# Eight of the down projection's 28 block products done by seven smaller products each: a second Strassen-Winograd level, in part

## The chip, the cores and the metric

One core of one Trainium2 chip. The metric is the device time of one execution in microseconds (us), lower is better.

## The reference

A linear attention block (A) and a gated block (B) run twice on 2048 tokens of width 1024. Only B's last matrix product, the down projection, changes:

```
x = x + A(layernorm(x));  x = x + B(layernorm(x));  x = x + A(layernorm(x));  x = x + B(layernorm(x))

def B(x, w_gate, w_up, w_down):          # D = 1024, F = 3584
    h = (x @ w_gate) * (x @ w_up)
    return h @ w_down                    # [2048, 3584] @ [3584, 1024]
```

Inputs and output are bfloat16.

## The kernel before

The kernel already uses one level of Strassen's scheme in Winograd's form: a product of 2x2 blocks is done with seven block products instead of eight, at the price of sums of blocks. Tokens are taken in two halves, so with two layers there are four **passes** of the down projection (I number them 1 to 4; each follows a gate/up stage), each with seven **products**, named in the order in which they run: 1, 2, 6, 7, 4, 5, 3. One product is [512 tokens x 1792] times [1792 x 512], 56 matmuls of 128x128 stationary (h) by 128x512 moving (weights). In code and traces PE is TensorE with its matmuls, PEld its weight loads, DVE VectorE, ACT ScalarE, POOL GpSimd; L1609 is line 1609 of the kernel; a bank is the part of PSUM into which the code sums a group of matmuls (`psb(bank)`); with a semaphore the program makes one engine wait for another. `...` marks cuts:

```python
DPROD = ["1", "2", "6", "7", "4", "5", "3"]
...
for qi, q in enumerate(DPROD):
    ...
    def grp(t, hf, ...):                    # t: 128 tokens, hf: half of the 14 slices of K
        bank = (B_DX if q in "1674" else B_DV)[t]
        P.add("pe", lambda e: [e.matmul(psb(bank), hv[:, 7 * hf + k, t * 128:(t + 1) * 128], w[:, k, :],
                                        start=(q in "15" and hf == 0 and k == 0), stop=(hf == 1 and k == 6), ...)
                               for k in range(7)], ...)
        if t == 3:
            ring_issue()                    # refill this weight slot
    for t in range(4):
        ...
        grp(t, 0); grp(t, 1)
        if q == "1":   ...  ACT copies the bank; DVE: hd += hc, ha = hd - ha
        elif q in "24": ... DVE: x = bank * CD + x
        elif q in "67": ... DVE: rtmp = bank * CD + x;  for 6 also hb -= ha, ha = hc - ha
        else:           ... DVE: x = bank * CD + rtmp
        ticks(q, t)                         # layernorm of the next stage, sums for the next pass
```

The program gives every engine its instructions in one fixed order; a helper works out which semaphores each must wait for. And `ha`, `hb`, `hd` are changed in place by VectorE in products 1 and 6, so in the program product 7 starts on a tile of tokens only when VectorE has got through its queue up to that tile.

## Time and profile before

| | before |
|---|---|
| time, median of 3 runs | 1462.43 us (1460.23 to 1463.21) |
| span of the profiled run | 1456.9 us |
| four passes, first to last start of their matmuls | 87.84, 88.51, 88.10, 88.10 us |
| spacing of starts, 128x512 (1553 pairs) / 128x256 (1884 pairs) | 0.2158 / 0.1092 us |

The engines' busy time from the page (busy us, share of the span, number of instructions):

```profile
PE 1437.1 (99%) x7850; PEld 755.1 (52%) x7850; DVE 1133.2 (78%) x2248; ACT 657.6 (45%) x1354; POOL 144.7 (10%) x176
```

Groups of the same trace: the down projection's matmuls, and below them, kept apart by shape, VectorE's sums of 1792 columns and the gate/up stage's half-width matmuls. The columns are busy us in all and mean ns of one, then the idle time of the engine just before them:

```profile
L1609 PE MATMUL ps<-arena 128*128 128x512 f16 (+1 forms) x1568 | 340.9, 379 | 0.0
...
L757 DVE TENSOR_TENSOR arena<-arena 128x1792 f16<-128x1792 f16 x64 | 69.0, 1084 | 1.2
...
L1392 PE MATMUL ps<-arena 128*128 128x256 f16 x2184 | 287.5, 273 | 1.9 <-DVE ps L1405 1.0 <-DMA arena<-sp_scratch 0.9
```

A matmul's 379 or 273 ns is its modelled length in the pipeline, not what it costs; what it costs in a stream is the spacing of the starts, 215.8 or 109.2 ns. The down projection's matmuls never wait: 0.0 us. In the chain of work that ended last each pass is a single piece (start us, length us, what), here the first and the last:

```profile
416.04 81.58 PE ps L1609 x378
...
1373.92 80.09 PE ps L1609 x371
```

So any matmul column taken out of a pass shortens the kernel by its own time, as long as nothing else becomes late. How busy the others are in the four passes shows in the windows (window, then its length and the busy us of each engine, with the number of instructions):

```profile
core 0: us, PE busy (x) PEld busy (x) DVE busy (x) ACT busy (x) POOL busy (x), PEclk, DMA share, GB/s
412.00:498.00 86.00, 86.00 (x400) 39.02 (x399) 45.47 (x59) 2.88 (x5) 4.67 (x4) 1.00 0.65 202
661.00:744.00 83.00, 83.00 (x388) 37.71 (x386) 57.09 (x92) 2.28 (x4) 11.11 (x21) 1.00 0.89 282
1121.00:1209.00 88.00, 88.00 (x415) 40.26 (x413) 47.52 (x64) 3.23 (x6) 4.67 (x4) 1.00 0.71 231
1367.00:1454.00 87.00, 86.99 (x408) 39.64 (x406) 37.96 (x49) 3.23 (x6) 0.00 (x0) 1.00 0.47 163
```

VectorE (DVE) is free for 26 to 49 us of each pass.

### The profile page before, as it was taken

How to read it: one execution, taken by the hardware profiler on the slowest of the kernel's cores; microseconds unless marked ns; L12 is line 12 of the kernel's file. 1: busy time of each engine (PE TensorE's matmuls, PEld its weight loads, DVE VectorE, ACT ScalarE, POOL GpSimd, SP SyncE). 2: the span in 40 equal slices, each digit the busy share in tenths (PEclk: the TensorE clock that was granted, in tenths of full speed). 3: DMA queues.
4: the chain of work that ended last, by engine and by line, in shares of the span. 5: the costliest groups of instructions: out<-in, count | busy, mean ns of one | idle time of the engine just before them, and what ended most of it. 6: DMA issues, size and time to landing. Idle time of an engine off the chain costs nothing.

```text
span 1456.9 us, 21047 instructions
## 1 busy us (share of the span) xinstructions
PE 1437.1 (99%) x7850; PEld 755.1 (52%) x7850; DVE 1133.2 (78%) x2248; ACT 657.6 (45%) x1354; POOL 144.7 (10%) x176
## 2 busy tenths in 40 slices
PE   8999998999999999999999999999999999999999
PEld 3444443455544466664444444446666445666544
DVE  6987977999964599987579878778888736888842
ACT  5673355444410166660047723567765004777400
POOL 2212521000010000001010045210000100000000
PEclk9999999999999999999999999999999999999999
DMA  8578977997785777768885166667776956777652
GB/s 260 88 202 224 214 177 153 301 302 269 258 269 187 244 255 247 258 238 266 257 267 137 58 169 163 173 177 258 259 243 202 328 190 225 260 257 252 224 185 94
DMA packets 270455, 320.17 MB, mean 220 GB/s; under 512 B 161936, under 2 KB 212880, under 8 KB 270352
## 3 DMA queue, kind: packets, MB, share of 16 engines
q1 hardware_dynamic: 270352, 318.82, 71.6%
q8 instruction: 62, 1.02, 0.3%
q14 instruction: 41, 0.34, 0.1%
HBM read 236.45 MB, written 73.40 MB: 213 GB/s over the span
## 4 chain that ended last, share of the span: by engine, by line
PE 86%; DVE 7%; DMA 3%; ACT 2%; issue 1%; POOL 1%; SPq 0%; ACTq 0%; DVEq 0%
PE ps L1311 27%; PE ps L1609 23%; PE ps L1392 16%; PE ps L1130 8%; PE ps L911 6%; PE ps L882 3%; PE ps L1232 2%; DMA arena<-arena 2%; DVE arena L443 2%; DVE arena L757 1%; DVE arena L604 1%; DMA arena<-in_A_wqkv_dram 1%; POOL arena L1013 1%; DMA arena<-sp_scratch 1%; PE ps L1156 0%
## 5 line engine op out<-in xcount | busy, mean ns | idle before, releaser
L757 DVE TENSOR_TENSOR arena<-arena 128x512 f16<-128x512 f16 (+10 forms) x951 | 430.2, 480 | 61.6 <-ACT arena L1396 34.1
L760 DVE SCALAR_TENSOR_TENSOR arena<-ps,arena 128x512 f16<-128x512 f32 (+2 forms) x497 | 336.3, 688 | 172.4 <-PE ps L1609 136.9
L1311 PE MATMUL ps<-arena 128*128 128x512 f16 x1888 | 457.3, 379 | 2.7 <-ACT ps L1340 2.0
L1609 PE MATMUL ps<-arena 128*128 128x512 f16 (+1 forms) x1568 | 340.9, 379 | 0.0
L1392 PE MATMUL ps<-arena 128*128 128x256 f16 x2184 | 287.5, 273 | 1.9 <-DVE ps L1405 1.0
L1311 PEld LDWEIGHTS ps<-arena 128*128 128x128 f16 (+1 forms) x1888 | 182.8, 98 | 165.6 <-ACT ps L1340 6.3
L1392 PEld LDWEIGHTS ps<-arena 128*128 128x128 f16 (+1 forms) x2184 | 212.1, 98 | 92.8 <-ACT arena L1396 6.9
L1609 PEld LDWEIGHTS ps<-arena 128*128 128x128 f16 x1568 | 153.4, 98 | 183.7
L1316 ACT ACTIVATE arena<-ps 128x512 f32<-128x512 f32 x224 | 133.7, 597 | 81.4 <-PE ps L1311 64.4
L1340 ACT COPY ps<-ps 128x512 f32<-128x512 f32 x112 | 65.4, 584 | 178.5 <-PE ps L1311 167.0
L1396 ACT ACTIVATE arena<-ps 128x256 f32<-128x256 f32 x351 | 125.1, 385 | 26.9 <-PE ps L1392 22.0
L911 PE MATMUL ps<-arena 128*128 128x512 f16 (+1 forms) x560 | 123.2, 379 | 2.7 <-ACT arena L918 0.9
L1130 PE MATMUL ps<-arena 128*128 128x512 bf16 x512 | 116.1, 379 | 0.0
L1232 PE MATMUL ps<-arena 128*128 128x512 bf16 x512 | 111.4, 379 | 3.6 <-ACT ps L1226 3.0
L446 POOL TENSOR_SCALAR arena<-arena 128x1 f32<-128x1 f32 x64 | 23.1, 360 | 810.3 <-DVE arena L445 810.3
L1402 ACT COPY ps<-ps 128x256 f32<-128x256 f32 x182 | 66.4, 365 | 75.0 <-DVE arena L760 28.3
L443 DVE BATCH_NORM_STATS2 arena<-arena 128x6 f32<-128x512 bf16 x128 | 88.2, 689 | 13.8 <-DMA arena<-in_A_x_dram 7.0
L1013 POOL TENSOR_TENSOR arena<-arena 128x1024 f16<-128x1024 f32 x32 | 75.3, 2354 | 183.4 <-DVE arena L1011 166.3
L911 PEld LDWEIGHTS ps<-arena 128*128 128x128 f16 x560 | 54.0, 98 | 70.9 <-ACT arena L918 5.1
L882 PE MATMUL ps<-arena 128*128 128x512 bf16 x384 | 85.5, 379 | 3.7 <-ACT arena L547 1.6
L1405 DVE TENSOR_TENSOR ps<-ps,arena 128x256 f32<-128x256 f32 x182 | 76.7, 428 | 10.5 <-PE ps L1392 9.6
L1232 PEld LDWEIGHTS ps<-arena 128*128 128x128 f16 x512 | 49.8, 98 | 64.8 <-ACT ps L1226 4.3
(56 smaller groups left out, 755.3 us busy)
## 6 DMA issues: line engine op xcount, KB each, us to landing
arena<-w_scratch SPq DMA_DIRECT2D x84, 896.0 KB, 4.6
arena<-t_scratch SPq DMA_DIRECT2D x32, 896.0 KB, 6.1
arena<-in_B_w_down_dram SPq DMA_DIRECT2D x24, 896.0 KB, 5.0
arena<-sp_scratch SPq DMA_DIRECT2D x26, 768.0 KB, 4.2
w_scratch<-arena SPq DMA_DIRECT2D x28, 512.0 KB, 6.2
arena<-w_scratch SPq DMA_DIRECT2D x28, 384.0 KB, 5.2
x_scratch<-arena SPq DMA_DIRECT2D x40, 256.0 KB, 7.6
arena<-x_scratch SPq DMA_DIRECT2D x40, 256.0 KB, 5.6
```

Source lines behind the costliest of these rows:

```text
L443: P.add("dve", (lambda h: lambda e: e.bn_stats(st[j][:, 6 * h:6 * h + 6], x_res[:, i, (D // 2) * h:(D // 2) * (h + 1)]))(h), rd=r_x(i, (D ...
L757: P.add("dve", lambda e: e.tensor_tensor(out=out, in0=a, in1=b, op=op), rd=rd, wr=wr, prd=prd)
L760: P.add("dve", lambda e: e.scalar_tensor_tensor(out=out, in0=a, scalar=sc, in1=b, op0=ALU.mult, op1=op1), rd=rd, wr=wr, prd=prd)
L882: return [e.matmul(psb(bank), xnT[:, k, i * 128:(i + 1) * 128], t[:, k, h * 512:(h + 1) * 512], start=(k == 0), stop=(k == KT - 1)) for k ...
L911: P.add("pe", lambda e: [e.matmul(psb(bank), a[0][:, k, :], b[0][:, k, :], start=(q in (1, 5) and k == 0), stop=(k == 3), skip_group_check ...
L1130: return [e.matmul(psb(bank), xrt[t][:, jj * 128:(jj + 1) * 128], pk[:, h, t, :], start=(t == tok[0]), stop=(t == tok[NST - 1])) for t in ts]
L1232: return [e.matmul(psb(bank), xnT[:, g, i * 128:(i + 1) * 128], wp[:, g, dh * 512:(dh + 1) * 512], start=(dh == 0 and g == 0), stop=(g == ...
L1311: P.add("pe", lambda e: [e.matmul(psb(bank), w[:, k, :], x[:, k, :], start=(start and k == 0), stop=(k == 3), skip_group_check=True) for k ...
L1316: P.add("act", lambda e: e.activation(t, psb(bank), AF.Copy, scale=SG), prd=[bank], wr=r)
L1392: P.add("pe", lambda e: [e.matmul(psb(bank)[:, 256 * half:256 * half + 256], w[:, k, :], xx[:, k, :], start=(start and k == 0), stop=(k == ...
L1396: P.add("act", lambda e: e.activation(d, src, AF.Copy, scale=sc), prd=[xk], wr=rd_)
L1609: P.add("pe", lambda e: [e.matmul(psb(bank), hv[:, 7 * hf + k, t * 128:(t + 1) * 128], w[:, k, :], start=(q in "15" and hf == 0 and k == 0 ...
```

## The change

Products 4 and 5 (passes 1 and 3), 5 (pass 2), and 4, 5 and 3 (pass 4), eight of the 28, are each done by seven sub-products again: 98 matmuls of 128x256 in place of 56 of 128x512, an eighth fewer columns. VectorE makes four sums of h (S1 to S4) and four of the weights (T1 to T4) ahead of time, each 128x1792, at points named in a schedule: "20" is after tile 0 of product 2, "4d" after step d of product 4, the steps being the twelve entries of `order`. The sub-results are put together in PSUM and SBUF by VectorE and ScalarE. The four sums of h's input for the next pass (`tq`) move from product 5 to product 3, because their buffers now hold S sums.

The diff, cut to its core (`...` marks cuts; buffers and the re-ordering of the plain branch into `evac` are left out):

```diff
+    L2DOWN = {(False, 0): "45", (False, 1): "5", (True, 0): "45", (True, 1): "453"}
+    DSCHED = {
+        "45": {"20": "S1:5 S1:4", "21": "S2:5 S2:4", "22": "S3:5 S4:4", "23": "S4:5", "70": "S3:4 T1:4", "72": "T2:4 T3:4", "73": "T1:5",
+               "4d": "T4:4", "4j": "T2:5", "4m": "T3:5", "5d": "T4:5"},
+        "5": {"20": "S1:5", "21": "S2:5", "22": "S3:5", "23": "S4:5", "41": "T1:5", "42": "T2:5", "43": "T3:5", "5d": "T4:5"},
+        "453": {"20": "S1:5 S1:4", ..., "23": "S4:5", "70": "S3:4 T1:4", "71": "S1:3", "72": "T2:4 T3:4", "73": "T1:5",
+                "4d": "T4:4", "4f": "S2:3", "4j": "T2:5", "4m": "T3:5", "5d": "T4:5 S4:3", "5h": "T1:3", "5k": "S3:3", "5m": "T2:3", "3d": "T3:3", "3f": "T4:3"},
+    }
...
+                    l2w[q] = dict(ops={"S1": (s1, a21, a22, ALU.add), "S2": (s2, s1, a11, ALU.subtract), "S3": (s3, a11, a21, ALU.subtract),
+                                       "S4": (s4, a12, s2, ALU.subtract), "T1": (t1, b12, b11, ALU.subtract), "T2": (t2, b22, t1, ALU.subtract),
+                                       "T3": (t3, b22, b12, ALU.subtract), "T4": (t4, b21, t2, ALU.subtract)},
+                                  mm={1: (a11, b11), 2: (a12, b21), 3: (s4, b22), 4: (a22, t4), 5: (s1, t1), 6: (s2, t2), 7: (s3, t3)}, done=[])
+                def l2_ops(q, step):
+                    for tk in sched.get(q + str(step), "").split():
...
+                        tt(o[0], a[0], b[0], op, a[1] + b[1], o[1])
...
+                    def mm(i, r, bank, half, start=False):
+                        (a, ra), (b, rb) = W["mm"][i]
+                        P.add("pe", lambda e: [e.matmul(psb(bank)[:, 256 * half:256 * half + 256], a[:, k, 128 * r:128 * r + 128], b[:, k, :],
+                                                        start=(start and k == 0), stop=(k == 6), skip_group_check=True) for k in range(7)], ...)
...
+                    def first_(r):
+                        mm(5, r, UB[r], 0, True)
+                        mm(1, r, UB[r], 1)
+                        if q == "5":
+                            P.add("act", ... r4 = copy of half 0 ...)
+                            put(r, r)                 # ACT: half 1 into the result's bank
+                        else:
+                            acc(r, 1, r, 0, rin)      # DVE: three half-width accumulations
+                            acc(r + 2, 1, r, 0, rin)
+                            acc(r, 0, r, 1, rin)
+                    def m6(r):
+                        mm(6, r, UB[r], 1)
+                        put5(r, r)  or  acc(r, 1, r, 1, rout)
+                    def m7(r):
+                        mm(7, r, UB[r], 1)
+                        put5(r + 2, r); put(r + 2, r)  or  two acc
...
+                    order = ((f, 0), (f, 1), (m2, 0), (m6, 0), (m2, 1), (m6, 1), (m7, 0), (m3, 0), (m7, 1), (m3, 1), (m4, 0), (m4, 1))
+                    for st_, (fn, r) in enumerate(order):
+                        fn(r)
...
+                        l2_ops(q, "abcdefghijkm"[st_])
...
-                if q == "5":
+                if q == "3" and t < 2:
+                    tq.pop(0)()
                     tq.pop(0)()
```

## The prediction

> **What bounds the kernel now.** TensorE's stream of matmuls. The engine table gives PE 99% of 1456.9 us, DVE 78%, ACT 45%; the chain that ended last is 86% PE. PE is never late in the stage that changes: the groups table gives the down projection's matmuls (1568 of 128x512) 0.0 us of idle before them, and the chain runs through each of the four passes as one unbroken piece of 80 to 82 us (about 412-497, 661-745, 1125-1210, 1371-1455 us). Starts in the timeline are 0.2158 us apart for a 128x512 matmul and 0.1092 us apart for a 128x256 one (gate/up stage, 1884 pairs, although each loads its own 128x128 weights, 98 ns). So halving the width costs only about 1% of the rate. [...]
>
> **Removed and added, per changed product.** Before: 56 matmuls x 0.2158 = 12.09 us of PE. After: 7 x 2 x 7 = 98 matmuls x 0.1092 = 10.70 us. Saved 1.39 us; eight products: 11.1 us, 0.76% of the span. All of it lies on the chain.
>
> Added on DVE: eight sums of 128x1792 f16; the same shape takes 1.08 us in the groups table (1.065 back to back), 8.6 us. Products 4 and 3 also need 12 half-width accumulations (a 128x512 one takes 0.69 us, so I estimate 0.42 us for 128x256, 0.36 back to back): 4.5-5 us. Product 5 needs four PSUM additions (0.43 us) and six ACT copies (0.37 us). In all about 69 + 19 + 7 = 95 us of DVE, lifting it to some 85% of the span. DMA traffic is unchanged, ring refills move by about 1 us, and the four half-transformed sums of the next pass (1.22 us each) move from product 5 to product 3.
>
> **Does DVE fit?** By windows, DVE is busy in the four passes about 39-44, 58, 47 and 37 us of 84. Added: 22, 10, 22 and 35. So it fits on average. Locally: product 2 of pass one gets 7.5 us of sums behind a DVE backlog that already lasts until 431 us; I get about 2 us of lag, absorbed in product 7, where DVE has 2.3 us of slack per tile. In the last pass products 4, 5 and 3 follow each other with 11-12, 9-10 and 10-11 us of DVE work in 10.7 us each, in order. Following the queue by hand, DVE enters product 3 about 3 us late, and PE then waits about 0.4 us before "m6" and 0.2 us before "m7". With semaphore latencies I expect 0.5-1.5 us of new PE waits in all, nearly all in the last pass. The gate/up start after a pass keeps its sp_scratch load (7.3 us in the chain, 1.1 us of PE idle at 1216).
>
> **Predicted:** 11.1 - about 1.1 = 10 us saved: 1452.3 us, 80% range 1448.5 to 1456.5. Within 2%: 0.97; faster by over 2%: 0.01; slower: 0.02.
>
> **What would show it.** 1120 instead of 1568 matmuls of 128x512 in the down projection and 784 new of 128x256 at 0.109 us spacing. Passes shorter by 2.8, 1.4, 2.8 and 3.5 us. DVE busy near 1228 us. New PE waits on DVE accumulations only in the last pass, after about 1420 us. ACT up by about 9 us.
>
> **What would make it wrong.** Stationary or strided operands slowing the half-width matmuls; each new sum being slower on strided sources; DVE backlog from product 4 stalling product 5; the T sums waiting for ring weights and blocking everything behind them on DVE; the next stage being DVE-bound (748-791 us) and giving the gain of pass two back.

A passage that did not come from this case's traces is cut from the prediction. No term of its sum stood in it: 11.1 us from the trace's spacings, less about 1.1 us, is 10 us. For the sizes that it estimates at 128x256, the trace of before has f32 sums of that width at 0.421 (L757) and 0.428 us (L1405), the latter with starts 0.331 us apart where one follows another. As to semaphore latencies, in the chain of before the step from a finished instruction to the one that waited for it ("issue") is for instance 0.02 us at 1219.53 and 0.05 us at 1221.69; that the new waits come to 0.5 to 1.5 us was an estimate. In the stage that it fears to be DVE-bound (748 to 791 us) the trace has VectorE busy for 39.4 of 43 us and PE for 41.6.

## The result

The median was 1450.3 us (1449.55 to 1453.15, 4 runs) against 1462.53 us (4 runs) of before. The ratio is 0.9923, with a 95% interval of 0.9905 to 0.9940. A ratio here is the mean time of one kernel's runs over the mean of the other's of the same rounds, so it is not quite the ratio of the two medians. It amounts to 11.3 us; two later timings of the same kernel gave 8.6 and 11.0 us (below). The prediction was 1452.3 us with a range of 1448.5 to 1456.5.

The page and the groups after, in the same order as before (line numbers have moved: 1736 is the plain product, 1654 the second-level one, 765 and 768 VectorE's two helpers):

```profile
PE 1426.2 (98%) x8186; PEld 787.3 (54%) x8186; DVE 1218.2 (84%) x2376; ACT 665.6 (46%) x1378; POOL 147.2 (10%) x176
```

```profile
L1736 PE MATMUL ps<-arena 128*128 128x512 bf16 (+1 forms) x1120 | 244.7, 379 | 0.0
...
L1654 PE MATMUL ps<-arena 128*128 128x256 f16 (+1 forms) x784 | 86.8, 273 | 0.5 <-DVE arena L768 0.3
```

```profile
L765 DVE TENSOR_TENSOR arena<-arena 128x1792 f16<-128x1792 f16 x124 | 132.6, 1082 | 1.2
...
L768 DVE SCALAR_TENSOR_TENSOR arena<-ps,arena 128x256 f32<-128x256 f32 x48 | 18.6, 420 | 3.4 <-PE ps L1654 2.5
```

448 of the 128x512 matmuls are gone and 784 of 128x256 have come: 784 x 0.1092 = 85.6 us of PE for 448 x 0.2158 = 96.7. VectorE gained 85.0 us, less than the 95 that were counted, because a sum that follows another directly starts before the first one's recorded end (two of the new sums in a row take 2.08 us in the timeline, not 2.16). The estimates for single operations held: 1.08 us for a sum and 0.42 us for a half-width accumulation.

The chain through the passes, now in pieces. In passes 1 and 2:

```profile
417.68 45.33 PE ps L1736 x210
463.00 21.40 PE ps L1654 x196
484.40 12.09 PE ps L1736 x56
...
662.50 55.90 PE ps L1736 x259
718.40 10.70 PE ps L1654 x98
729.10 12.09 PE ps L1736 x56
```

A plain product takes 12.09 us, a second-level one 10.70 us, and the change from one to the other costs nothing. In pass 3 the chain goes to VectorE and comes back only in the middle of product 4:

```profile
1171.20 0.60 DVE arena L768
1171.81 1.00 DVE arena L765
1172.81 1.01 DVE arena L768 x3
1173.81 0.05 issue
1173.86 17.75 PE ps L1654 x161
1191.61 12.10 PE ps L1736 x56
```

And in pass 4:

```profile
1413.26 15.30 PE ps L1654 x140
...
1429.01 1.99 DVE arena L765 x2
...
1432.33 1.00 DVE arena L765
1433.32 0.35 DVE ps L1670
...
1433.70 0.36 ACT ps L1667
...
1434.11 7.07 PE ps L1654 x63
```

A long stretch of VectorE in the chain does not mean that PE stood still all that time. It says who released the instruction that was late; how late is read from the gap between the starts of PE's matmuls. Less the normal spacing, those gaps are 0.47 us before 1173.86, 0.39 us before 1434.11 and 0.16 us before 1441.16: 1.02 us in all.

The windows of the passes:

```profile
412.00:497.00 85.00, 85.00 (x493) 47.98 (x492) 67.29 (x91) 4.89 (x11) 4.67 (x4) 1.00 0.68 212
661.00:742.00 81.00, 81.00 (x426) 41.57 (x425) 65.95 (x103) 4.29 (x10) 13.00 (x22) 1.00 0.94 294
1119.00:1204.00 85.00, 84.69 (x495) 48.12 (x494) 68.05 (x95) 5.24 (x12) 4.67 (x4) 1.00 0.73 238
1366.00:1446.00 80.00, 79.69 (x514) 49.81 (x512) 69.83 (x99) 4.29 (x10) 0.00 (x0) 1.00 0.51 175
```

Where the time went, as us from the first to the last matmul start of a stage:

| stage | before | after | difference |
|---|---|---|---|
| start to pass 1 | 409.40 | 411.04 | +1.64 |
| pass 1 (products 4, 5) | 87.84 | 85.07 | -2.77 |
| gate/up between | 157.58 | 157.57 | -0.01 |
| pass 2 (product 5) | 88.51 | 87.12 | -1.39 |
| between | 376.66 | 376.71 | +0.05 |
| pass 3 (4, 5) | 88.10 | 85.81 | -2.29 |
| gate/up between | 157.42 | 157.72 | +0.30 |
| pass 4 (4, 5, 3) | 88.10 | 84.60 | -3.50 |
| last matmul to the end | 3.26 | 3.50 | +0.24 |

The passes give 9.95 us. (Pass 4 now ends on a narrow matmul, whose own 0.109 us lie outside this measure, where 0.216 us did before; with them the passes give 10.06 us, which is 8 x 1.386 less the 1.02 us of waits.) The first row is not the change: the stage before pass 1 took between 408.0 and 412.8 us in the thirteen traces, with no relation to the kernel. The 0.30 us is the known start of a gate/up stage that waits for a load from sp_scratch (PE idle 1.11 us before, 1.42 us after); e1, whose matmuls are those of before, took 158.46 us there, so this too is variation. This spread of the first stage is why the spans of two single traces differ by 7.7 us and not by 10, and why the timing needs many runs for a figure that the pass lengths give at once.

In the traces of e1 to e11, all but e4, the record of each pass's first matmul is missing (a pass then has, for instance, 471 records of 476, and starts 0.216 us late); pass lengths quoted below have 0.216 us added for that.

### The profile page after: what moved, and what is told of

It is laid out like the page before. It is cut to its first block, busy times and chain, and to the rows that moved or that the text cites. A ratio compares the mean times of both kernels' runs of the same rounds, so it can differ in the third digit from the quotient of the medians.

```text
span 1449.1 us, 21876 instructions
## 1 busy us (share of the span) xinstructions
PE 1426.2 (98%) x8186; PEld 787.3 (54%) x8186; DVE 1218.2 (84%) x2376; ACT 665.6 (46%) x1378; POOL 147.2 (10%) x176
## 4 chain that ended last, share of the span: by engine, by line
PE 80%; DVE 11%; DMA 4%; issue 2%; ACT 2%; POOL 1%; SPq 1%; POOLq 0%; DVEq 0%; ACTq 0%
PE ps L1319 27%; PE ps L1400 16%; PE ps L1736 14%; PE ps L919 6%; PE ps L1138 6%; PE ps L1654 5%; DVE arena L765 3%; PE ps L890 3%; DMA arena<-arena 3%; PE ps L1240 2%; DVE arena L451 2%; DVE arena L768 1%; DVE arena L1015 1%; DVE arena L1012 1%; DVE arena L612 1%
## 5 line engine op out<-in xcount | busy, mean ns | idle before, releaser
L765 DVE TENSOR_TENSOR arena<-arena 128x512 f16<-128x512 f16 (+8 forms) x1015 | 497.8, 518 | 61.6 <-ACT arena L1404 33.6
L768 DVE SCALAR_TENSOR_TENSOR arena<-ps,arena 128x512 f16<-128x512 f32 (+3 forms) x545 | 353.6, 664 | 68.7 <-PE ps L1736 26.9
L1736 PE MATMUL ps<-arena 128*128 128x512 bf16 (+1 forms) x1120 | 244.7, 379 | 0.0
L1736 PEld LDWEIGHTS ps<-arena 128*128 128x128 f16 x1120 | 109.6, 98 | 130.2
L919 PE MATMUL ps<-arena 128*128 128x512 f16 (+1 forms) x560 | 123.2, 379 | 2.7 <-ACT arena L926 0.9
L1682 ACT COPY arena<-ps 128x256 f32<-128x256 f32 x8 | 3.0, 372 | 197.1 <-PE ps L1654 197.1
L919 PEld LDWEIGHTS ps<-arena 128*128 128x128 f16 x560 | 54.0, 98 | 70.9 <-ACT arena L926 5.1
L1654 PE MATMUL ps<-arena 128*128 128x256 f16 (+1 forms) x784 | 86.8, 273 | 0.5 <-DVE arena L768 0.3
```

The lines of the kernel that those rows point to most:

```text
L765: P.add("dve", lambda e: e.tensor_tensor(out=out, in0=a, in1=b, op=op), rd=rd, wr=wr, prd=prd)
L768: P.add("dve", lambda e: e.scalar_tensor_tensor(out=out, in0=a, scalar=sc, in1=b, op0=ALU.mult, op1=op1), rd=rd, wr=wr, prd=prd)
L919: P.add("pe", lambda e: [e.matmul(psb(bank), a[0][:, k, :], b[0][:, k, :], start=(q in (1, 5) and k == 0), stop=(k == 3), skip_group_check ...
L1654: P.add("pe", lambda e: [e.matmul(psb(bank)[:, 256 * half:256 * half + 256], a[:, k, 128 * r:128 * r + 128], b[:, k, :], start=(start and ...
```

## The experiments

The theory: the gain is columns taken off a TensorE stream that has no waits, 1.39 us per product, and the 85 us added to VectorE are hidden in its slack. Rivals: (R1) part of the gain comes from the rest of the diff, such as the moved sums; (R2) the added VectorE work costs PE time, which the shorter matmuls then more than pay; (R3) the narrow matmuls do not run at their share of the rate. A further question is what decides when VectorE's work begins to cost: its total, or its place in the queue.

### e1_none: the new code without any second-level product

```diff
-    L2DOWN = {(False, 0): "45", (False, 1): "5", (True, 0): "45", (True, 1): "453"}
+    L2DOWN = {(False, 0): "", (False, 1): "", (True, 0): "", (True, 1): ""}
     DSCHED = {
+        "": {},
```

> The changed code with no product on the second level; the four half-transformed sums stay moved to the last product. Theory (the gain is matmul columns taken off TensorE): the time of before, 1462.5 us within 0.2%, and four passes of 87.8, 88.5, 88.1 and 88.1 us in the trace, as before. Rival (the moved sums or the re-ordered code bring part of the gain): clearly below 1460 us, or passes shorter than before.

Measured: 1459.86 us median of 5 against 1460.6 us of before on the same chip, ratio 0.9999 (0.9985 to 1.0012). Passes 87.85, 88.51, 88.10, 88.10 us: those of before. R1 is out; the moved sums and the rest of the diff are worth nothing by themselves. (The "clearly below 1460" of the expectation was set for a chip on which before takes 1462.5; against this chip's 1460.6 the ratio decides.)

### e2_again: the changed kernel timed again

No edit.

> The changed kernel once more, timed in more rounds. Theory: 11 to 12 us below before, and the same passes of 85.1, 87.1, 85.8 and 84.6 us (to 0.1 us) in a second trace, so that what differs between the traces outside the passes (1.6 us in the first 410 us) is variation between runs. Rival (the first stage really is 1.6 us slower in the changed kernel): again about 411 us from the start to the first pass.

Measured: ratio 0.9941 (0.9927 to 0.9954), 8.6 us; medians 1451.2 against 1460.6. Less than the 11 to 12 expected. Passes 85.07, 87.12, 86.18, 84.60 us. Three of the four repeat to 0.01 us. Pass 3 differs by 0.37: its wait in product 4 was 0.66 us this time, and there was another of 0.18 us before it (the cause is found under e11). The stage before pass 1 took 408.2 us, less than in the trace of before, so the first row of the table above is variation.

### e4_halves: narrow matmuls alone

The kernel before, with each matmul of a product split in two halves of 256 columns:

```diff
-[e.matmul(psb(bank), hv[...t...], w[:, k, :], ...) for k in range(7)]
+[e.matmul(psb(bank)[:, 256 * h:256 * h + 256], hv[...t...], w[:, k, 256 * h:256 * h + 256], ...) for h in range(2) for k in range(7)]
```

> The kernel before, with every down-projection matmul of 128x512 split into two of 128x256 (3136 instead of 1568), same sums, same weights loaded twice as often. Theory (a half-width matmul costs 0.1092 us against 0.2158, so the narrow width costs 0.0026 us per pair): 1568 x 0.0026 = 4.1 us slower, each pass longer by 1.0 us. Rival (more weight loads or more instructions cost more than the spacing in the gate/up stage shows): more than 6 us slower.

Measured: ratio 1.0017 (1.0004 to 1.0030), 2.5 us; passes 88.93, 89.60, 89.17, 89.17 us, longer by 1.07 to 1.09 each and 4.3 us together (3.9 us with the own length of each pass's last matmul, now a narrow one, on both sides; 4.1 were counted). The interval of the timing is 0.6 to 4.4 us. Twice as many weight loads do no harm:

```profile
L1609 PE MATMUL ps<-arena 128*128 128x256 f16 (+1 forms) x3136 | 344.8, 273 | 0.0
...
L1609 PEld LDWEIGHTS ps<-arena 128*128 128x128 f16 x3136 | 306.7, 98 | 37.6
```

A load takes 98 ns and a half-width matmul 109 ns, so the load just fits behind the matmul. R3 is out: the price of the narrow width is about 1.2% of a pass, as counted.

### e5_only5: one product per pass

```diff
+    L2DOWN = {(False, 0): "5", (False, 1): "5", (True, 0): "5", (True, 1): "5"}
```

> Only product 5 on the second level, in all four passes: four products instead of eight. Theory (1.39 us per product, independent of each other): each pass 1.39 us shorter than before (86.45, 87.12, 86.71, 86.71), together 5.55 us; timed about 5 to 6 us below before. Rival (the gain comes from something that any second-level product brings at once, or the other products cost as much as they give): more than 8 or less than 3 us.

Measured: ratio 0.9949 (0.9923 to 0.9974), 7.5 us with an interval of 3.8 to 11; medians 1454.4 against 1462.5. The timing alone does not tell 5.5 from 8. The passes do: 86.46, 87.13, 86.72, 86.71 us, each 1.38 or 1.39 below before, 5.5 us together, with no PE wait. The products are independent of each other, and each is worth what its columns are worth.

### e7_sums: VectorE's sums alone

All 64 sums are made, at nearly the same points, but the matmuls stay those of before. So that the result stays right, S3 and T3 write into the finished S1 and T1 in place of h and the weights:

```diff
+    # letters of the schedule become the tiles of the plain product; run_l2 is not called
-    "S3": (s3, a11, a21, ALU.subtract)   ...   "T3": (t3, b22, b12, ALU.subtract)
+    "S3": (s1, a11, a21, ALU.subtract)   ...   "T3": (t1, b22, b12, ALU.subtract)
```

> All 64 sums of the second level on VectorE (69 us), but the matmuls and evacuations of before; the results of the sums are not used. Theory (VectorE's slack hides them): within 1.5 us of before, passes within 0.5 us of before's. Rival (the added VectorE work costs TensorE time that the shorter matmuls then more than pay back): over 3 us slower than before.

Measured: correct; ratio 0.9978 (0.9957 to 0.9998), if anything faster, which I take for the noise of these rounds. Passes 87.85, 88.51, 88.10, 88.10 us: no longer than before by even 0.02 us, with VectorE 62.6 us busier (1195.8 against 1133.2):

```profile
PE 1435.4 (98%) x7788; PEld 755.2 (52%) x7850; DVE 1195.8 (82%) x2312; ACT 658.0 (45%) x1354; POOL 146.1 (10%) x176
```

For the sums R2 is out. What this run leaves aside is the accumulations of the second level, and that the second-level matmuls wait for the sums while the plain ones do not. For these R2 is settled by the trace of the changed kernel: all the PE time lost in its passes is the 1.02 us of gaps above.

### e6_last45: product 3 of the last pass back to plain

```diff
-(True, 1): "453"
+(True, 1): "45"
```

> The changed kernel with products 4 and 5 instead of 4, 5 and 3 in the last pass. Theory (product 3 saves 1.39 us and its sums cost 0.54 us of PE waits there): the last pass is 85.3 us, 0.7 to 0.85 us longer than the changed kernel's 84.6, with no PE wait in it; the tail after the last matmul shrinks by 0 to 0.3 us. Rival (product 3 is not worth its sums): last pass no longer than 84.7 us.

Pass 4 is 85.33 us, that is 88.10 less 2 x 1.386, with no wait in it. So in the changed kernel product 3 brings 85.33 - 84.60 = 0.73 us by this measure, and 0.84 us with the last matmul's own length (0.216 or 0.109 us) added on both sides: 1.39 less the 0.54 us of waits that come with it. Still worth having, at some 60% of its value. The time from the last matmul to the end was 3.25 us (after: 3.50).

### e8_double: six of eight sums twice

```diff
-                        tt(o[0], a[0], b[0], op, a[1] + b[1], o[1])
+                        for _ in range(1 if nm in ("S3", "T3") else 2):
+                            tt(o[0], a[0], b[0], op, a[1] + b[1], o[1])
```

> The changed kernel with six of the eight sums of each product computed twice (48 more, 51 us of VectorE). Theory (VectorE has slack left in pass 2, little in 1 and 3, none in the last): pass 2 unchanged within 0.2 us, passes 1 and 3 longer by 1 to 4 us each, the last by 5 to 12 us; 8 to 20 us slower than the changed kernel in all. Rival (VectorE still has slack everywhere, as 84% busy suggests): under 3 us slower.

Measured: ratio to before 1.0142 (1.0116 to 1.0169); 1483.86 us, some 30 us slower than the changed kernel. Passes 92.1, 89.0, 97.4, 95.2 us: longer than the changed kernel's by 7.0, 1.9, 11.6 and 10.6 us. My sizes were too small in every pass but the last, and the rival is out, although VectorE was still not full on average: the page has it at 86%. Not all of the 11.6 us of pass 3 need be the sums' doing: ahead of any doubled sum of this pass VectorE waited 5.51 us for a DMA, against 4.29 us in the changed kernel (see e11). In pass 3, 7.8 us of the loss is one wait at the start of product 7, in the timeline of PE:

```profile
1164.66 1.89 PE L1737 MATMUL ps<-arena 128*128 128x512 f16 x8
1174.17 14.71 PE L1737 MATMUL ps<-arena 128*128 128x512 f16 x56 [7.62 <-DVE arena L765]
1188.72 3.98 PE L1655 MATMUL ps<-arena 128*128 128x256 f16 x35
1194.13 17.95 PE L1655 MATMUL ps<-arena 128*128 128x256 f16 x161 [1.43 <-DVE arena L768]
```

The second line also shows a loss that I had not counted: 56 matmuls took 14.71 us, not 12.25 (55 x 0.2158 + 0.379). Their first twelve are spaced 0.43 us, half the rate. After the wait of 7.8 us the half rate lasts 5 us, and the granted clock from 1174 to 1179 us is 0.50 (0.94 in the whole window of 1125 to 1215 us). After waits of 4.3 and 4.0 us (in passes 4 and 1, whose windows have a granted clock of 0.98) five or six matmuls run at full rate and then 3.4 to 3.6 us of them at half (0.213 us for 256 columns). After a wait of 2.6 us the spacing stays normal, as it does after the longest in the traces of before and after, 1.99 and 1.98 us (0.216 us for 512 columns). Why the clock falls these runs do not show.

### e11_double2: twice, but only the sums in product 2

```diff
+                        for _ in range(2 if q == "2" and nm != "S3" else 1):
```

> The changed kernel with only the sums that stand in product 2 computed twice: 6 more in passes 1, 3 and the last, 3 more in pass 2, 22 us of VectorE in all against 51 us in e8. Theory (what costs time is VectorE's backlog at one place, in order, not the total): pass 3, where the backlog is longest when product 2 ends, waits 3 to 6 us before product 7, pass 1 0 to 2 us, pass 2 and the last under 0.5 us. Rival (the loss in e8 went with the total of VectorE work): about 22/51 of e8's loss in every pass, 3, 0.8, 5 and 4.5 us.

Passes 86.97, 88.92, 94.25, 84.60 us, longer than the changed kernel's by 1.9, 1.8, 8.1 to 8.4 and 0.0. Pass 3 pays more than the 6.4 us of work that was added to it (6 x 1.065), because PE's wait of 6.35 us is followed by twelve matmuls at half rate, another 2.6 us lost (56 matmuls in 14.84 us, not 12.25), 8.9 us in all:

```profile
1164.86 14.84 PE L1737 MATMUL ps<-arena 128*128 128x512 f16 x56 [6.18 <-DVE arena L765]
```

Pass 4 got the same six sums and pays nothing. So the rival, the total, falls: it wanted 4.5 us there. What counts is the backlog in VectorE's queue at the point where PE next needs it. In pass 4 VectorE has no backlog when product 2 ends (no layernorm runs there; in the changed kernel's trace it idles 1.33 us at that point). In pass 3 it does (there it has no pause from 1142.9 to 1176.2 us). I had the sign right for pass 3, its size too small (I expected 3 to 6), and pass 2 wrong (1.8, not under 0.5).

The origin of pass 3's backlog is seen in the changed kernel's chain: a layernorm operation of VectorE at 1137.76 waits for a DMA, and VectorE starts nothing of what stands behind it in the program until then.

```profile
1130.95 6.72 DMA arena<-arena
...
1137.76 0.55 DVE arena L471
```

VectorE idles 4.29 us there, and 4.10 us at the same place in the trace of before, without consequence; VectorE's timelines have, after and before:

```profile
1137.76 0.55 DVE L471 TENSOR_SCALAR arena<-arena 128x1024 f16<-128x1024 bf16 x1 [4.29 <-DMA arena<-arena]
...
1140.06 0.55 DVE L463 TENSOR_SCALAR arena<-arena 128x1024 f16<-128x1024 bf16 x1 [4.10 <-DMA arena<-arena]
```

No run removes this wait, but it varies by itself, and four traces have the same code in pass 3. Where VectorE waits 4.19, 4.29, 4.29 and 4.67 us for the DMA (e6, after, e10, e2), PE's waits in the pass are 0.38, 0.47, 0.47 and 0.84 us: they grow by as much as the DMA wait does. Pass 1, with the same schedule and no such DMA wait, has no PE wait. In the changed kernel's timeline of pass 3 VectorE's operations stand in the order of the program (2, 2, 2, 1 sums behind the tiles of product 2 and 2, 0, 2, 1 behind those of product 7, as scheduled).

### e3_tuned and e9_tuned2: moving single sums

In the changed kernel's pass 3, T1 of product 5 stands just before the three accumulations that PE waits for, though it is needed only some 9 us later. In pass 4, VectorE idles 1.77 us at the start of product 5 and is late at its end. So I moved sums:

```diff
 e3:  "45":  T1:5 from "73" to "4j"
      "453": S4:3 from "5d" to "5a", T1:3 from "5h" to "5b", T2:3 from "5m" to "5h", T3:3 from "3d" to "5m", T4:3 from "3f" to "3d"
 e9:  as e3, but T1:5 to "4f" and T2:3 to "5i"
```

> The changed kernel with five sums moved: T1 of product 5 out of the way of product 4's first accumulations (passes 1 and 3), and S4, T1, T2, T3 of product 3 into VectorE's idle stretch at the start of product 5 (last pass). Theory (the waits are VectorE queue order, not its total work): the three PE waits of 0.47, 0.39 and 0.16 us go, passes of 85.1, 87.1, 85.3 and 84.05 us; about 1 us below the changed kernel, which the timing will hardly resolve. Rival (VectorE is simply full there): the waits stay or move elsewhere, pass lengths within 0.2 us of the changed kernel's.

Measured e3: passes 85.53, 87.13, 85.78, 84.44 us. The old waits of pass 3 and of product 3 are gone. T1 at "4j" came too late, and product 5 now waits 0.45 us for it, in pass 1 too; and in pass 4 T2 at "5h" held up the last PSUM addition just as T1 had, 0.39 us again. Ratio 0.9927 (0.9915 to 0.9940).

> The second try at placing the sums: T1 of product 5 after product 4's step f (not j), T2 of product 3 after product 5's step i (not h), the rest as in e3_tuned. Theory (e3's remaining waits were its own, from T1 placed just before the matmuls that read it and from T2 placed just before a PSUM addition that a matmul waits for): no PE wait over 0.05 us in any pass; passes of 85.07, 87.12, 85.33 and 83.94 us, which is before less 1.386 us per product; 1 us below the changed kernel, hardly resolved by timing. Rival (VectorE is full in these products, and a wait removed in one place comes back in another): a wait of 0.3 us or more in pass 3 or the last.

> The changed kernel on the same chip as e9. Theory: passes of 85.07, 87.12, 85.8 to 86.2 and 84.60 us, waits in pass 3 (0.5 to 0.9 us) and in the last (0.39 and 0.15 us); 11 us below before. Rival: none; it is the yardstick for e9.

Measured on one chip: e9 1449.31 us (ratio 0.9925, 0.9912 to 0.9937), the changed kernel as e10 1448.86 us (ratio 0.9925, 0.9913 to 0.9937). By time they are the same. By pass: e10 has 85.07, 87.12, 85.81, 84.60 us with waits of 0.47, 0.39 and 0.15 us again, e9 has 85.07, 87.12, 85.33, 84.42 us. Pass 3 now has no wait and its full 2.77 us, so there the wait was a matter of order. (VectorE's DMA wait was 4.13 us in e9's trace. By the four traces above some 0.3 us of PE wait would have been left in the old order; that is an estimate.) In pass 4 the two waits are gone and another, of 0.36 us, has come in product 3, where the chain of e9 reads:

```profile
...
1435.84 1.00 DVE arena L765
1436.83 1.01 DVE arena L768 x3
...
1437.89 2.14 PE ps L1654 x18
```

From 1427.9 to the end VectorE hardly pauses. For pass 4 the rival holds in both orders tried: VectorE is nearly full across products 5 and 3, and a wait taken away in one place comes back in another. That no order is free of waits is not shown. (The 83.94 us expected of it left out that the last matmul is narrow; without any wait it would be 84.05.) e9 gains 0.66 us over e10 in the passes, which is 0.05% and too little for the timing; it is not shown to be the faster kernel.

## Why the prediction was right

- **What bounds it.** Right. e1 and e5 show that the time falls with the columns and with nothing else in the diff, and every stage outside the passes keeps its length.
- **1.39 us per product.** Right to 0.01 us: 12.09 against 10.70 us in the chain, and 5.5 us for four products in e5. The key was to take the cost of a 128x256 matmul from spacings in this kernel's own trace (0.1092 us, against 0.2158 us at 512 columns).
- **VectorE hides its new work.** Right: e7 adds 62.6 us to it and no pass grows. The estimates of the single operations were right; their sum was 10 us too high, because back to back they overlap (64 sums of 1.08 us raised VectorE's busy time by 0.98 us each in e7).
- **0.5 to 1.5 us of new waits.** Right in the sum, 1.02 us, but partly by luck, since almost half of it arose where none was counted. "New PE waits on DVE accumulations only in the last pass" was wrong: 0.47 us (0.84 us in e2) is in pass 3. The step that failed there was to follow the queue by hand only in passes 1 and 4 and to let pass 3 pass for a copy of pass 1. In pass 3 a layernorm operation waits 4.3 us for a DMA, which the trace of before showed as harmless idle time; it became backlog when sums were queued behind it, and the PE wait grew with it from trace to trace (e11). In pass 4 I expected 0.4 us before "m6" and 0.2 us before "m7" of product 3. The second came (0.16 us). In place of the first there were 0.39 us in product 5, where "m4" waits for a ScalarE copy behind a VectorE addition.
- **Lag in pass 1.** I had about 2 us absorbed in product 7; VectorE had caught up by 451 us, late in product 6.
- **The time.** 1452.3 us predicted, 1450.3 us measured, against 1462.4 and 1462.5 us of before. The passes show 10.0 us where I had 10. Three timings of the changed kernel give 11.3, 8.6 and 11.0 us, so the mechanism accounts for the gain within what the timing resolves.

What stays open: why the stage before pass 1 varies by some 5 us from run to run, why VectorE's DMA wait in pass 3 varies, and how much VectorE work each pass could still take; e8 and e11 show that the answer depends on where it is put, and the sizes that I worked out by hand for them were too small.

## What to carry to other kernels

Where the trace shows an engine's stream without waits, the gain of taking work out of it can be counted from the spacing of its own instructions (5.55 us counted and 5.5 measured in e5), and lengths of stages that have no waits show it to 0.1 us where whole timings scatter by several. Whether added work on another engine is free is not a matter of its share of busy time (at 82% of the span e7 cost nothing, at 86% e8 cost some 30 us): follow that engine's queue in order to the next point where the bound engine needs it, and look for an old idle wait ahead of that point, since here one of 4.1 us turned into backlog. Keep what the bound engine needs next in front of what it needs later, and expect that in a stretch where the helper is nearly full a removed wait may only move, as it did here in pass 4.
